# A gated attention loop feeding two experts: the order of three engines taken from tables of steps, two logarithms in one instruction, a state updated in place

## Chip, cores, metric

The kernel runs on one core of one Trainium2 chip. The metric is the device time of one execution in microseconds (us), as the median of the runs shown. A profiled execution has two times of its own: the run's time, and the span of its trace, from which all rows below come.

## What is computed

A complex-gated linear attention over 4 batches, 8 heads, 768 positions and a head size of 48 is followed by a router and a two-layer network per token.

```python
mag = np.sqrt(a_re * a_re + a_im * a_im)
scale = np.minimum(mag, 0.999) / (mag + 1e-06)
for t in range(S):
    # per head: complex state, decayed by the gate, plus the outer product of k and v
    S_re, S_im = ar * S_re - ai * S_im + kv, ar * S_im + ai * S_re
    y[:, :, t] = np.einsum('bhd,bhde->bhe', q[:, :, t], S_re)
...
logits = x @ w_gate + modality_bias[modality_id]      # x: y with the heads side by side, 3072 x 384
e_idx = np.argmax(logits, axis=1)                      # one expert per token, gate_w its softmax weight
h = np.maximum(x[mask] @ w1[e], 0.0)
out[mask] = gate_w[mask, None] * (h @ w2[e])
```

## The kernel before

**Units and pairs.** The 768 positions are cut into G = 6 chunks of 128. A unit n is one chunk of one batch with all heads; there are 24, ordered by chunk, then by batch. Two units of neighbouring batches form a pair x; there are 12. The gate is worked on by pairs, with tiles of 128 x 768 (one half) or 128 x 1536 (both halves); the attention is worked on by units.

**Gate of a pair.** ScalarE squares both parts of the gate (`squares`, L132), VectorE makes their product `tan`, the sign `neg` and the sum of squares; ScalarE takes two logarithms of 128 x 768 (`logs`, L143: the squared modulus into its own tile `lm`, the squared real part in place) and two exponentials (`tangents`, L151: the reciprocal, and `off`, the small correction for the 1e-06); VectorE finishes the tangent and the cut at 0.999. After an arctangent (L164) TensorE sums the angles over the chunk with triangular matrices (`angles`, L167, result `u`), VectorE adds the angle carried from the chunk before and takes the fraction of a turn (`fractions`, L185), ScalarE makes sine and cosine into `css` (`waves`, L205). TensorE sums the logarithms (`sums`, L213, result `ls`), and ScalarE makes the modulus and its reciprocal, `pm` (`moduli`, L222). Row 127 of angle and modulus goes to memory and comes back as the carry `cb` (L182) and as the factor `mt` of the state (L240).

**Attention of a unit.** VectorE makes `qkp` = q,k times `pm`, and `QK` = `qkp` times `css` (`hats`, L243). TensorE turns both into `tKT`, `tQT`; ScalarE copies them out (`turned`, L266). In `inner` (L281) TensorE makes the scores `wp`, VectorE masks them into `W`; TensorE makes the two state additions `up`; VectorE makes `mid` (state after the first half chunk), `U` and the new state `U` x `mt`. In `outer` (L313) TensorE makes `yp` from `W` and the values and from the states; ScalarE copies it to `yT`. In `rows` (L331) TensorE multiplies `yT` by `sel`, which gives rows of tokens and the router's logits (`xw`); ScalarE writes the rows `xr`, VectorE sums the logits `lg`, and a DMA writes the rows to memory (L344).

**Table sets.** Logarithm and exponential are in one table set of ScalarE (EXP), arctangent and sine in another (TRIG); `table` (L103) loads a set. In the loop each pair takes one load of either.

**PSUM.** All of TensorE's results, and those of router and experts, are taken from one pool of four double banks (`pair`, L66). A result's buffer is free when its last reader is done.

**What sets the order.** The loop over turns w (L396 on) writes the steps in program order: pairs run up to five pairs ahead of the units. A planner orders the instructions of each engine from program order, dependences and costs of its own. Only ScalarE's activations and table loads are held in program order (`then`, L98); its copies, and all work of TensorE and VectorE, go where the planner puts them. SP issues nearly all DMAs, in one queue.

**Router and experts.** `beside(w, place)` is called at four places of each turn. It releases one scatter of rows at a time on the GpSimd queue (L636) and, from turn 18 on, parts of the first three expert tiles by a plan of turns and places (`Layers.PLAN`, L745). The router takes the logits in five portions (`takes`), the last after unit 23. After the loop the remaining expert tiles follow (`run`, L887): 12 tiles of 256 rows and one of 128, each with 24 matmuls to `h_ps` in two parts and 8 per 128 rows to `y_ps`. Tiles after the first seven need the places of all rows, so they wait for the last portion.

Of the kernel before, what the change touches and what calls it, by code (L numbers as in the profile page):

```python
# [20 lines left out]
ET = mybir.EngineType  # L21


def gate_loop(nc, ctx, tc, cpool, ident, q, k, v, a_re, a_im, sel, lg, x_rows, make_router, make_layers):
# [71 lines left out]
    chain = []  # L96

    def then(ins):  # L98
        if chain:
            tc.add_manual_dep(ins.ins, chain[-1].ins.name, mybir.DependencyInfo(mybir.DependencyClass.NoSync, mybir.DependencyReason.DATA), reason="order of the table sets")  # L100
        chain.append(ins)

    def table(name):  # L103
        then(nc.scalar.preload_act_table_set(name))  # L104

    def act(*args, **kw):
        then(nc.scalar.activation(*args, **kw))  # L107
# [24 lines left out]
    def squares(x):  # L132
        ab = box.pop(("ab", x))
        sq = el.tile([L, 2, NG, H, D], F32, name="sq", bufs=1)
        act(sq[:], ab, Act.Square)
        tan = el.tile([L, NG, H, D], F32, name="tan", bufs=2)
        nc.vector.tensor_tensor(tan[:], ab[:, 0], ab[:, 1], Alu.mult)
        neg = el.tile([L, NG, H, D], BF16, name="neg", bufs=2)
        nc.vector.tensor_scalar(neg[:], ab[:, 0], 0.0, None, Alu.is_lt)
        nc.vector.tensor_tensor(sq[:, 1], sq[:, 0], sq[:, 1], Alu.add)  # L140
        box["squares", x] = sq, tan, neg

    def logs(x):  # L143

        sq, tan, neg = box["squares", x]
        lm = el.tile([L, NG, H, D], F32, name="lm", bufs=3)
        act(lm[:], sq[:, 1], Act.Ln)
        act(sq[:, 0], sq[:, 0], Act.Ln)
        box["logs", x] = lm

    def tangents(x):  # L151
# [10 lines left out]
        box["lm", x] = lm, off  # L162

    def arctans(x):  # L164
        act(box["tangents", x][0][:], box["tangents", x][0][:], Act.Arctan)

    def angles(x):  # L167

        tan, neg = box.pop(("tangents", x))
        us = pair([L, H, D], "u")  # L170
        for i in range(NG):
            nc.tensor.matmul(us[:, i], turn[:], tan[:, i], start=True, stop=False)  # L172
            nc.tensor.matmul(us[:, i], halfb[:], neg[:, i], start=False, stop=True)
        box["angles", x] = us

    def carries(x):

        g, b = groups[x][0]
        if g:
            cb = el.tile([L, NG, H * D], F32, name="cb")  # L180
            n0 = (g - 1) * B + b
            nc.sync.dma_start(out=cb[:], in_=f_scr[n0:n0 + NG][None].broadcast_to([L, NG, H * D]))  # L182
            box["carry", x] = cb

    def fractions(x):  # L185

        us = box.pop(("angles", x))
        g, b = groups[x][0]
        f = el.tile([L, NG, H, D], F32, name="f")
        r = el.tile([L, NG, H, D], F32, name="r", bufs=1)  # L190
        if g:
            cb = box.pop(("carry", x))
            nc.vector.tensor_tensor(f[:], us, cb[:].rearrange("p i (h d) -> p i h d", d=D), Alu.add)
            nc.vector.tensor_scalar(r[:], f[:], ROUND, -ROUND, Alu.add, Alu.add)
            nc.vector.tensor_tensor(f[:], f[:], r[:], Alu.subtract)
        else:
            nc.vector.tensor_scalar(r[:], us, ROUND, -ROUND, Alu.add, Alu.add)
            box["last"] = nc.vector.tensor_tensor(f[:], us, r[:], Alu.subtract)
# [3 lines left out]
        nc.vector.tensor_scalar(r[:].bitcast(I32), f[:].bitcast(I32), 0x7FFFFFFF, None, Alu.bitwise_and)  # L202
        box["fractions", x] = f, r

    def waves(x):  # L205

        f, r = box.pop(("fractions", x))
        cs = css[:, x % 2]
        act(cs[:, :, :, 1, :], f[:], Act.Sin, scale=2.0 * math.pi)
        act(cs[:, :, :, 0, :], r[:], Act.Sin, scale=-2.0 * math.pi, bias=quarter[:])  # L210
        box["cs", x] = cs

    def sums(x):  # L213

        lm, off = box.pop(("lm", x))
        ls = pair([L, H, D], "ls")
        for i in range(NG):
            nc.tensor.matmul(ls[:, i], half[:], lm[:, i], start=True, stop=False)  # L218
            nc.tensor.matmul(ls[:, i], nhalfb[:], off[:, i], start=False, stop=True)
        box["sums", x] = ls  # L220

    def moduli(x):  # L222
        ls = box.pop(("sums", x))
        pm = el.tile([L, 2, NG, H, D], F32, name="pm")
        act(pm[:, 1], ls, Act.Exp)
        act(pm[:, 0], ls, Act.Exp, scale=-1.0)
        g, b = groups[x][0]
        if g < G - 1:
            n0 = g * B + b
            nc.sync.dma_start(out=m_scr[n0:n0 + NG].rearrange("i h d -> (i h d)")[None], in_=pm[L - 1:L, 1].rearrange("o i h d -> o (i h d)"))  # L230
        box["pm", x] = pm

    def decays(x):

        g, b = groups[x][0]
        if g < G - 1:
            n0 = g * B + b
            mt = mts[x % 4]
            for part in (mt[0:D], mt[64:64 + D]):
                nc.sync.dma_start(out=part, in_=m_scr[n0:n0 + NG].rearrange("i h d -> d i h"))  # L240
            box["mt", x] = mt

    def hats(w):  # L243

        if not 0 <= w < NU or (hats, w) in done:
            return
        done.add((hats, w))
        x, i = w // NG, w % NG
        cs = box["cs", x]
        pm = box["pm", x]  # L250
        qk = box["qk", x]
        qkp = un.tile([L, 2, H, D], F32, name="qkp", bufs=1)
        nc.vector.tensor_tensor(qkp[:], qk[:, :, i], pm[:, :, i], Alu.mult)
        QK = QKs[w % 4]
        wave = cs[:, i].rearrange("p h c d -> p (h c d)")[:, None, :].broadcast_to([L, 2, H * 2 * D])
        twice = qkp[:].rearrange("p a h d -> p (a h) d")[:, :, None, :].broadcast_to([L, 2 * H, 2, D])
        box["hat"] = nc.vector.tensor_tensor(QK[:, :, :, :, 0:D].rearrange("p a h c d -> p (a h c) d"), wave, twice, Alu.mult)  # L257
        box["hats", order[w]] = QK

# [106 lines left out]
    for x in range(2):  # L366
        phase(load_a, x)
# [658 lines left out]
```

## Time and profile before

| | us |
|---|---|
| median of 3 runs | 333.12 (331.14 to 333.34) |
| the profiled execution: its own time | 336.16 |
| the profiled execution: span of its trace | 334.5 |
| busy in the span: TensorE / its weight loads | 264.3 / 208.5 |
| busy in the span: VectorE / ScalarE / GpSimd | 236.4 / 235.2 / 74.9 |

Rows of a timeline give start, duration, engine, line, operation, output and input, count, and in square brackets how long the engine had been idle and what ended it. Rows of windows give a stretch of the span and how long each engine was busy in it, the granted TensorE clock (1.00 is full), the busy share of the 16 DMA engines and the rate. PE is TensorE, PEld its weight loads, DVE is VectorE, ACT ScalarE, POOL GpSimd, SPq the DMA queue of SyncE. A cycle below is the stretch from one EXP load to the next, that is one pair and two units.

### The profile page before, as it was taken

How to read it: one execution, taken by the hardware profiler on the slowest of the kernel's cores; microseconds unless marked ns; L12 is line 12 of the kernel's file. 1: busy time of each engine (PE TensorE's matmuls, PEld its weight loads, DVE VectorE, ACT ScalarE, POOL GpSimd, SP SyncE). 2: the span in 40 equal slices, each digit the busy share in tenths (PEclk: the TensorE clock that was granted, in tenths of full speed). 3: DMA queues.
4: the chain of work that ended last, by engine and by line, in shares of the span. 5: the costliest groups of instructions: out<-in, count | busy, mean ns of one | idle time of the engine just before them, and what ended most of it. 6: DMA issues, size and time to landing. Idle time of an engine off the chain costs nothing.

```text
span 334.5 us, 12364 instructions
## 1 busy us (share of the span) xinstructions
PE 264.3 (79%) x5300; PEld 208.5 (62%) x5300; DVE 236.4 (71%) x437; ACT 235.2 (70%) x291; POOL 74.9 (22%) x110
## 2 busy tenths in 40 slices
PE   0034649779879888978988899999898989899950
PEld 0012438648577776768785878889786767576730
DVE  1619989999998989899898978794452274336510
ACT  2786999999998989979897979534434446432420
POOL 8200000000000000000433323153045148633440
PEclk9999698999989999997999999999999999999995
DMA  8996886969888778695998873927634342644220
GB/s 137 187 187 104 166 168 100 149 91 165 181 182 158 152 142 172 132 181 109 137 240 161 188 159 95 142 77 115 67 65 113 73 129 81 123 94 131 82 90 7
DMA packets 172152, 43.74 MB, mean 131 GB/s; under 512 B 162978, under 2 KB 168484, under 8 KB 172088
## 3 DMA queue, kind: packets, MB, share of 16 engines
q1 hardware_dynamic: 166456, 32.60, 55.7%
q0 software_dynamic: 5632, 10.26, 12.9%
q8 instruction: 43, 0.70, 0.9%
q14 instruction: 21, 0.17, 0.2%
HBM read 33.96 MB, written 9.77 MB: 131 GB/s over the span
## 4 chain that ended last, share of the span: by engine, by line
PE 35%; ACT 24%; DVE 11%; SPq 10%; DMA 8%; issue 6%; POOL 2%; ACTq 1%; POOLq 0%; DVEq 0%
PE h_ps L846 6%; ACT sq L107 5%; SPq L817 4%; PE wp L290 4%; ACT L104 4%; PE y_ps L866 4%; PE up L298 3%; PE yp L327 3%; ACT pm L107 3%; PE xw L336 3%; PE ls L218 3%; PE tQT L274 3%; DMA abs<-in_a_im_dram 2%; PE tKT L274 2%; ACT css L107 2%
## 5 line engine op out<-in xcount | busy, mean ns | idle before, releaser
L636 POOL DMA_INDIRECT x_slots<-xr,to x24 | 31.4, 1307 | 208.6 <-DVE mid L302 147.9
L257 DVE TENSOR_TENSOR QK<-css,qkp 128x1536 f32<-128x1536 f32 x24 | 42.1, 1755 | 0.4
L172 PE MATMUL u<-tan,turn 128*128 128x384 f32 x48 | 22.5, 554 | 23.1 <-ACT tan L107 22.9
L846 PE MATMUL h_ps<-xgT,w1t 128*128 128x256 bf16 (+1 forms) x312 | 35.7, 268 | 1.4 <-DMA xgT<-x_slots 1.4
L866 PE MATMUL y_ps<-w2t,hT 128*128 128x384 bf16 x200 | 35.8, 326 | 1.1 <-ACT hT L849 0.7
L882 POOL DMA_INDIRECT out_dram<-y_sb,idx x25 | 26.7, 1070 | 34.4 <-ACT y_sb L880 16.9
L846 PEld LDWEIGHTS <-w1t 128*128 128x128 bf16 x312 | 29.3, 98 | 6.4 <-issue 1.8
L104 ACT ACT_TABLE_LOAD x25 | 32.1, 1283 | 1.4 <-PEq L1010 0.9
L880 ACT ACTIVATE y_sb<-y_ps,own 128x384 f32<-128x384 f32 x25 | 13.2, 577 | 26.5 <-PE y_ps L866 23.0
L290 PEld LDWEIGHTS wp<-QT,KT 128*64 128x64 f32 x768 | 26.4, 146 | 8.3 <-issue 2.3
L290 PE MATMUL wp<-QT,KT 128*64 128x64 f32 x768 | 30.0, 234 | 2.0 <-ACT ex L107 1.4
L849 ACT ACTIVATE hT<-h_ps 128x1024 bf16<-128x1024 f32 (+1 forms) x20 | 20.0, 1002 | 14.3 <-PE h_ps L846 11.3
L275 ACT COPY KT<-tKT 128x1024 f32<-128x1024 f32 x24 | 24.3, 1012 | 8.1 <-PE tKT L274 5.0
L336 PE MATMUL xw<-sel,yT 128*128 128x104 f32 x192 | 27.0, 284 | 2.1 <-ACT QT L275 1.2
L274 PE MATMUL tKT<-ident,QK 64*128 64x64 f32 x384 | 18.3, 240 | 12.9 <-DVE QK L257 11.4
L298 PE MATMUL up<-V,QK 64*64 64x48 f32 x1408 | 28.1, 221 | 0.0
L866 PEld LDWEIGHTS <-hT 128*128 128x128 bf16 x200 | 18.3, 98 | 14.9 <-issue 2.1
L274 PEld LDWEIGHTS tKT<-ident,QK 64*128 64x128 f32 x384 | 15.0, 148 | 18.7 <-issue 13.9
L298 PEld LDWEIGHTS up<-V,QK 64*64 64x64 f32 x1408 | 25.1, 135 | 1.8 <-DVE lg L342 0.2
L172 PEld LDWEIGHTS u<-tan,turn 128*128 128x128 f32 x48 | 9.0, 214 | 27.4 <-issue 25.6
L336 PEld LDWEIGHTS xw<-sel,yT 128*128 128x128 f32 x192 | 23.4, 191 | 3.9 <-ACT QT L275 1.3
L275 ACT COPY QT<-tQT 128x1024 f32<-128x1024 f32 x24 | 24.5, 1023 | 0.3 <-PE tQT L274 0.3
(153 smaller groups left out, 548.3 us busy)
## 6 DMA issues: line engine op xcount, KB each, us to landing
abs<-in_a_re_dram SPq DMA_DIRECT2D x24, 192.0 KB
abs<-in_a_im_dram SPq DMA_DIRECT2D x24, 192.0 KB
qk<-in_q_dram SPq DMA_DIRECT2D x24, 192.0 KB
qk<-in_k_dram SPq DMA_DIRECT2D x24, 192.0 KB
V<-in_v_dram SPq DMA_DIRECT2D x24, 192.0 KB
cb<-f_scr SPq DMA_DIRECT2D x10, 384.0 KB
x_rows<-xr SPq DMA_DIRECT2D x24, 96.0 KB
abs<-in_moe_w_dram POOLq DMA_DIRECT2D x2, 768.0 KB
```

The source lines that it names most:

```text
L104: then(nc.scalar.preload_act_table_set(name))
L107: then(nc.scalar.activation(*args, **kw))
L172: nc.tensor.matmul(us[:, i], turn[:], tan[:, i], start=True, stop=False)
L257: box["hat"] = nc.vector.tensor_tensor(QK[:, :, :, :, 0:D].rearrange("p a h c d -> p (a h c) d"), wave, twice, Alu.mult)
L274: nc.tensor.transpose(tp[:, s, h], QK[rows_, i, h].rearrange("t c d -> t (c d)"), ident[rows_, rows_])
L275: box["turned QK"] = nc.scalar.copy(to[:], tp)
L290: nc.tensor.matmul(wp[rows_, h, :], KT[:, s, h], QT[:, s, h], start=True, stop=True)
L298: nc.tensor.matmul(up[to_c, s, h], QK[rows_, 0, h, c], V[rows_, h, 0:D], start=True, stop=True)
L336: nc.tensor.matmul(xw[:, j], yT[:, j], sel[:, j], start=True, stop=True)
L636: put = self.nc.gpsimd.indirect_dma_start(out=self.x_slots, out_offset=bass.IndirectOffsetOnAxis(ap=to, axis=0), in_=self.xr[m // 4 * 4][: ...
L846: nc.tensor.matmul(h_ps[:, f // nf, f % nf, :], w1t[:, k, ff * 128:(ff + 1) * 128], xgT[:, k, :], start=(k == 0), stop=(k == KD - 1))
L866: nc.tensor.matmul(y_both[:, s], self.hT[n][:, f, s * 128:(s + 1) * 128], w2t[:, f, :], start=(f == 0), stop=(f == NF - 1))
```

## The change

The functions for phases of a pair and stages of a unit are split into 42 single steps. Two strings name them: FRONT once, with absolute pair and unit numbers, CYCLE for x = 0 to 12, with numbers relative to pair x or unit 2x; steps out of range or already done are skipped. `then` now keeps one chain each for TensorE, ScalarE (copies among them) and VectorE, so the steps of each of these engines run in the order of the strings. What router and experts issue is in no chain, but for activations given to `act`.

Further: both logarithms of a pair are one instruction of 128 x 1536 in place (`ln`; pairs 0 and 1 keep two halves, `la`, `lb`), and the cut at 0.999 reads `sq` and writes `lm`. `U` goes straight into the new state's tile, and `nw` multiplies it in place; the tile `U` is gone. FRONT has 24 matmuls of bf16, 128 x 512, on constants (`warm`), whose result nobody reads, in no chain. The EXP load at the start is no longer written. Gate loads of pair x + 2 are issued when square, product and sign of pair x have been issued; q and k of pair x + 2 after `qkp` of pair x's second unit; values of unit n + 4 after `yV` of unit n; the carry's load right behind the write it reads, and so the load of `mt`. `beside` is called at steps `turn:u.p`, with the same turns and places.

The core of the diff:

```diff
+FRONT = """
+    sq:0 sum:0 tan:0 lb:0 neg:0 la:0 off:0 mn:0 e:0 tan2:0 ls0:0 TRIG warm:24 at:0 u0:0 sq:1 neg:1 sum:1 ls1:0 u1:0 EXP la:1 r:0 tan:1
+    lb:1 f2:0 e:1 ab:0 ep:0 v:0 off:1 tan2:1 em:0 TRIG s:0 qkp:0 mn:1 c:0 qk:1 tan:2 sq:2 QK:0 v:1 sum:2 at:1 tQ:0 ls0:1 EXP u0:1 ln:2
+    qkp:1 cQ:0 neg:2 tK:0 v:2 ls1:1 e:2 QK:1 tan2:2 off:2 cK:0 u1:1 mn:2 sq:3 r:1 sum:3 W:0 f2:1 ep:1 neg:3 em:1 tQ:1 up:0 ln:3 qkp:2
+    e:3 off:3 TRIG s:1 mask:0 mid:0 U:0 tan:3 mn:3 at:2 u0:2 ab:1 u1:2 c:1 tan2:3 sq:4 QK:2 f:2 sum:4 r:2 neg:4 f2:2 at:3 cQ:1 tK:1 v:3
+    cK:1 tan:4 ab:2 s:2 u0:3 u1:3 c:2
+"""
+
+CYCLE = """
+    xw:-1 turn:0.0 f:+3 qkp:+3 r:+3 up:+1 tK:+2 xr:-1 lg:-1 mid:+1 f2:+3 EXP cK:+2 ls0:+2 turn:0.1 ls1:+2 ln:+4 ep:+2 yV:+0 turn:0.2
+    U:+1 QK:+3 em:+2 yS:+0 neg:+5 tan:+5 yT:+0 W:+1 turn:0.3 e:+4 tK:+3 cK:+3 up:+2 turn:1.0 tQ:+2 off:+4 mask:+1 qkp:+4 xw:+0 tan2:+4
+    mid:+2 U:+2 nw:+1 yV:+1 turn:1.1 yS:+1 mn:+4 tQ:+3 turn:1.2 TRIG cQ:+2 ab:+3 xr:+0 W:+2 nw:+0 at:+4 yT:+1 sq:+5 lg:+0 cQ:+3 u0:+4
+    turn:1.3 s:+3 QK:+4 mask:+2 sum:+5 c:+3 u1:+4
+"""
 
...
-    chain = []
-
-    def then(ins):
-        if chain:
-            tc.add_manual_dep(ins.ins, chain[-1].ins.name, mybir.DependencyInfo(mybir.DependencyClass.NoSync, mybir.DependencyReason.DATA), reason="order of the table sets")
-        chain.append(ins)
+    chain = {}
+
+    def then(engine, *made):
+        if engine in chain:
+            tc.add_manual_dep(made[0].ins, chain[engine].ins.name, mybir.DependencyInfo(mybir.DependencyClass.NoSync, mybir.DependencyReason.DATA), reason="order of the steps")
+        chain[engine] = made[-1]
+        return made[-1]
 
     def table(name):
-        then(nc.scalar.preload_act_table_set(name))
+        then("act", nc.scalar.preload_act_table_set(name))
 
     def act(*args, **kw):
-        then(nc.scalar.activation(*args, **kw))
+        return then("act", nc.scalar.activation(*args, **kw))
+
+    def copy(*args):
+        return then("act", nc.scalar.copy(*args))
+
+    def vec(made):
+        return then("vec", made)
 
     order = [(g, b) for g in range(G) for b in range(B)]
...
-    def squares(x):
-        ab = box.pop(("ab", x))
-        sq = el.tile([L, 2, NG, H, D], F32, name="sq", bufs=1)
-        act(sq[:], ab, Act.Square)
-        tan = el.tile([L, NG, H, D], F32, name="tan", bufs=2)
-        nc.vector.tensor_tensor(tan[:], ab[:, 0], ab[:, 1], Alu.mult)
-        neg = el.tile([L, NG, H, D], BF16, name="neg", bufs=2)
-        nc.vector.tensor_scalar(neg[:], ab[:, 0], 0.0, None, Alu.is_lt)
-        nc.vector.tensor_tensor(sq[:, 1], sq[:, 0], sq[:, 1], Alu.add)
-        box["squares", x] = sq, tan, neg
-
-    def logs(x):
-
-        sq, tan, neg = box["squares", x]
-        lm = el.tile([L, NG, H, D], F32, name="lm", bufs=3)
-        act(lm[:], sq[:, 1], Act.Ln)
-        act(sq[:, 0], sq[:, 0], Act.Ln)
-        box["logs", x] = lm
-
-    def tangents(x):
-
-
-        sq, tan, neg = box.pop(("squares", x))
-        lm = box.pop(("logs", x))
+    def parts_read(x):
+
+        if all((part, x) in done for part in ("sq", "tan", "neg")):
+            box.pop(("ab", x))
+            load_a(x + 2)
+
+    def sq(x):
+        box["sq", x] = to = el.tile([L, 2, NG, H, D], F32, name="sq", bufs=1)
+        act(to[:], box["ab", x], Act.Square)
+
...
+    def ln(x):
+
+        sq = box["sq", x]
+        act(sq[:], sq[:], Act.Ln)
+
+    def part_ln(x, i):
+        part = box["sq", x][:, i]
+        act(part, part, Act.Ln)
+
+    def e(x):
+        sq = box["sq", x]
         act(sq[:, 0], sq[:, 0], Act.Exp, scale=-1.0)
-        off = el.tile([L, NG, H, D], BF16, name="off", bufs=2)
-        act(off[:], lm[:], Act.Exp, scale=-0.5, bias=ln_eps[:])
-        nc.vector.tensor_tensor(tan[:], tan[:], sq[:, 0], Alu.mult)
-        nc.vector.tensor_scalar(lm[:], lm[:], 2.0 * math.log(0.999), None, Alu.min)
-        box["tangents", x] = tan, neg
...
+    def mn(x):
+        box["lm", x] = to = el.tile([L, NG, H, D], F32, name="lm", bufs=3)
+        vec(nc.vector.tensor_scalar(to[:], box["sq", x][:, 1], 2.0 * math.log(0.999), None, Alu.min))
+
...
+    def logsum(x, i):
+
+        if i == 0:
+            box["ls", x] = pair([L, H, D], "ls")
+        ls = box["ls", x][:, i]
+        then("pe", nc.tensor.matmul(ls, half[:], box["lm", x][:, i], start=True, stop=False), nc.tensor.matmul(ls, nhalfb[:], box["off", x][:, i], start=False, stop=True))
...
+            for part in (0, 64):
+                nc.sync.dma_start(out=mts[x % 4][part:part + D], in_=m_scr[n0:n0 + NG].rearrange("i h d -> d i h"))
...
+        if i and x + 2 < NX:
+            load_qk(x + 2)
...
-            U = un.tile([C, H, D], F32, name="U")
-            nc.vector.tensor_tensor(U[:], mid[:], ups[1], Alu.add)
-            new = un.tile([C, H, D], F32, name=f"state{b}", bufs=2)
-            nc.vector.tensor_tensor(new[:], U[:], box["mt", (g * B + b) // NG][:, b % NG, :, None].broadcast_to([C, H, D]), Alu.mult)
-            state[b] = new
...
+    def U(n):
+        if more(n):
+            to = box["new", n] = un.tile([C, H, D], F32, name=f"state{order[n][1]}", bufs=2)
+            vec(nc.vector.tensor_tensor(to[:], box["states", n][1][:], box["up", n][:, 1], Alu.add))
+
+    def nw(n):
+        if more(n):
+            to = state[order[n][1]] = box.pop(("new", n))
+            vec(nc.vector.tensor_tensor(to[:], to[:], mts[n // NG % 4][:, n % NG, :, None].broadcast_to([C, H, D]), Alu.mult))
...
+        values(n + 4)
...
+    def step_of(name, n):
+
+        made, end = (A, NX) if name in A else (N_, NU)
+        if 0 <= n < end and (name, n) not in done:
+            done.add((name, n))
+            made[name](n)
+            if name in ("sq", "tan", "neg"):
+                parts_read(n)
...
-    table(EXP)
-    for x in range(2):
-        phase(squares, x)
-        phase(load_a, x + 2)
-        phase(logs, x)
-        phase(tangents, x)
-    table(TRIG)
-    for x in range(2):
-        phase(arctans, x)
-        phase(angles, x)
-    phase(fractions, 0)
-    with tc.issue_after(box["last"].ins):
-        phase(squares, 2)
-    phase(waves, 0)
-    phase(load_qk, 1)
...
+    def run(names, x):
+
+        for step in names.split():
+            name, _, n = step.partition(":")
+            if name == "EXP":
+                if x + 2 < NX:
+                    table(EXP)
+                for made in late:
+                    made(act)
+                late.clear()
+            elif name == "TRIG":
+                if x + 3 < NX:
+                    table(TRIG)
+            elif name == "turn":
+                beside(2 * x + int(n[0]), int(n[2]))
+            elif name == "warm":
+                idle = pair([128, 4, L], "idle")
+                for i in range(int(n)):
+                    nc.tensor.matmul(idle[:, i % 2], nhalfb[:], halfb[:, None, :].broadcast_to([L, 4, L]), start=True, stop=True)
+            elif name in ("qk", "v"):
+                (load_qk if name == "qk" else values)(int(n))
+            else:
+                step_of(name, (x if name in A else 2 * x) + int(n))
+
+    run(FRONT, 0)
+    for x in range(NX + 1):
+        run(CYCLE, x)
     for f in late:
         f(act)
     return open_[-1], layers

```

More of the change, by code (lines that the diff above doesn't have):

```diff
@@ L164, in arctans @@
[L164 to L174, printed above, removed]
+    def parts_read(x):
+        if all((part, x) in done for part in ("sq", "tan", "neg")):
+            box.pop(("ab", x))
+            load_a(x + 2)
@@ L176, in carries @@
     def carries(x):
+        if x < 2 or x >= NX:
+            return
         g, b = groups[x][0]
[L179 to L187, printed above, removed]
-        g, b = groups[x][0]
[L189 to L198, printed above, removed]
+        cb = el.tile([L, NG, H * D], F32, name="cb")
@@ L331, in rows @@
[L331 to L342 removed]
+            nc.sync.dma_start(out=m_scr[n0:n0 + NG].rearrange("i h d -> (i h d)")[None], in_=box["pm", x][L - 1:L, 1].rearrange("o i h d -> o (i h d)"))
```

325 lines of the change are left out of this document (143 added, 182 removed).

## The prediction

> **What bounds the kernel now.** I read the table loads on ScalarE first, to cut the span into cycles, then the busy time of each engine in the seven cycles from one EXP load to the next (57.89 to 177.08).
>
> ```profile
> 57.89:73.51 15.62, 11.66 (x233) 8.45 (x232) 15.62 (x23) 15.36 (x18) 0.00 (x0) 1.00 0.78 117
> 73.51:88.12 14.61, 13.73 (x376) 11.13 (x374) 14.53 (x24) 14.52 (x19) 0.00 (x0) 1.00 0.90 174
> 88.12:103.71 15.59, 13.11 (x368) 11.31 (x369) 15.42 (x23) 15.50 (x19) 0.00 (x0) 0.89 0.93 181
> 103.71:121.70 17.99, 15.81 (x415) 12.98 (x415) 16.45 (x24) 16.56 (x20) 0.00 (x0) 1.00 0.76 145
> 121.70:139.56 17.86, 16.02 (x417) 13.15 (x417) 16.40 (x28) 16.57 (x20) 0.00 (x0) 1.00 0.75 146
> 139.56:158.89 19.33, 16.41 (x420) 13.94 (x420) 18.23 (x49) 16.82 (x21) 0.24 (x1) 0.91 0.76 143
> 158.89:177.08 18.19, 16.95 (x422) 13.99 (x422) 17.21 (x31) 16.47 (x21) 7.03 (x6) 1.00 0.99 179
> sum 119.19, PE 103.69 PEld 84.95 DVE 113.86 ACT 111.79 POOL 7.27; mean PE 14.81 PEld 12.14 DVE 16.27 ACT 15.97 POOL 1.04
> ```
>
> The columns after the length are TensorE, its weight loads, VectorE, ScalarE, GpSimd, granted clock, DMA share, GB/s. Three engines are nearly full at once: VectorE 113.86 and ScalarE 111.79 of 119.19, TensorE 103.69. The first three cycles are short because they hold less unit work (233 to 376 matmul records against 415). The next are the full ones: near 18 with 16.5 of work on each of two engines, so 1.4 per cycle is handover. One such handover is a wait of TensorE for a free PSUM buffer (it needs no `yT` to turn `tQT`):
>
> ```profile
> 115.86 0.71 PE L274 MATMUL tQT<-ident,QK 64*128 64x64 f32 x16 [1.28 <-ACT yT L328]
> ```
>
> Behind the cycles the bound is another engine:
>
> ```profile
> 177.08:237.00 59.92, 54.64 (x1419) 46.09 (x1419) 46.39 (x114) 41.96 (x55) 18.10 (x15) 1.00 0.73 133
> 237.00:290.00 53.00, 50.56 (x641) 39.21 (x636) 22.22 (x65) 24.34 (x34) 25.39 (x25) 1.00 0.35 91
> ```
>
> TensorE is busy 91% and 95%: there it sets the pace, and the change removes no matmul. So I cost three stretches: up to the EXP load of cycle 0 (57.89), seven cycles to the EXP load of cycle 7 (177.08), and the rest.
>
> **The front.** ScalarE is the engine to add up, from these steps (start to next start):
>
> ```profile
> 7.82 1.48 ACT L107 ACTIVATE sq<-abs 128x1536 f32<-128x1536 f32 x1 [5.59 <-DMA abs<-in_a_im_dram]
> ...
> 57.89 1.28 ACT L104 ACT_TABLE_LOAD   x1
> ```
>
> ```profile
> 109.24 1.51 ACT L107 ACTIVATE pm<-ls 128x768 f32<-128x768 f32 x2 [0.38 <-PE ls L219]
> 110.64 0.85 ACT L107 ACTIVATE lm<-sq 128x768 f32<-128x768 f32 x1
> 111.37 1.72 ACT L107 ACTIVATE sq<-sq 128x768 f32<-128x768 f32 x2
> 112.99 0.92 ACT L107 ACTIVATE off<-lm,ln_eps 128x768 bf16<-128x768 f32 x1
> 113.93 1.28 ACT L104 ACT_TABLE_LOAD   x1
> 115.22 0.58 ACT L328 COPY yT<-yp 128x512 f32<-128x512 f32 x1
> ...
> 116.08 0.86 ACT L107 ACTIVATE tan<-tan 128x768 f32<-128x768 f32 x1
> 116.82 1.01 ACT L275 COPY KT<-tKT 128x1024 f32<-128x1024 f32 x1
> 117.71 1.03 ACT L275 COPY QT<-tQT 128x1024 f32<-128x1024 f32 x1
> 118.62 0.88 ACT L107 ACTIVATE css<-f 128x768 f32<-128x768 f32 x1
> 119.36 0.95 ACT L107 ACTIVATE css<-r,quarter 128x768 f32<-128x768 f32 x1
> 120.19 1.50 ACT L107 ACTIVATE sq<-abs 128x1536 f32<-128x1536 f32 x1
> 121.70 1.28 ACT L104 ACT_TABLE_LOAD   x1
> ```
>
> FRONT puts on ScalarE 5 squares at 1.5 (7.5), 4 half logarithms at 0.73 (2.9), 2 whole ones taken as a square (3.0), 4 reciprocals at 0.81 (3.2), 4 `off` at 0.94 (3.8), 4 arctangents at 0.74 (3.0), 3 sines and 3 cosines at 0.74 and 0.83 (4.7), 2 x 1.40 for `pm`, 4 copies at 0.90 (3.6) and 7 table loads at 1.29 (9.0): 43.5. Seven, because five are written and no load of the EXP set stands ahead of pair 0's logarithms any more: I take one to be put in before the logarithm and one before the exponential. From 7.82 that gives 51.3. Laying VectorE's steps beside it, I find the last sine due about 1.3 too early for its `f2`, so 52.6 instead of 57.89, if nothing else is late. FRONT has one copied unit and one `yT` less behind it, which the cycles below make up.
>
> [...]
>
> `warm` has no row. Its nearest are a bf16 matmul of 384 columns and the first sums of angles, cold and warm:
>
> ```profile
> L866 PE MATMUL y_ps<-w2t,hT 128*128 128x384 bf16 x200 | 35.8, 326 | 1.1 <-ACT hT L849 0.7
> ```
>
> ```profile
> 21.90 1.62 PE L172 MATMUL u<-tan,turn 128*128 128x384 f32 x2 [21.90 <-ACT tan L107]
> ...
> 26.39 0.81 PE L172 MATMUL u<-tan,turn 128*128 128x384 f32 x2
> ```
>
> 24 x 0.326 x 512/384 = 10.4 at most, on an engine that had nothing before 21.90; the constants are ready early, the first `u` is due near 17. If it keeps the clock up, two sums gain 0.8 each, which ScalarE's order hides. If the planner puts it behind the first `ls` instead, near 14.5, `u` comes up to 8 late, of which up to 5 reach ScalarE. I take 0, and keep -1 to +5.
>
> **The cycle.** VectorE does the same work in another order. What an order can save there stands in four rows:
>
> ```profile
> 107.95 0.55 DVE L139 TENSOR_SCALAR neg<-abs 128x768 bf16<-128x768 f32 x1
> 108.42 0.55 DVE L194 TENSOR_SCALAR r<-f 128x768 f32<-128x768 f32 x1
> 109.00 0.96 DVE L195 TENSOR_TENSOR f<-f,r 128x768 f32<-128x768 f32 x1
> 110.00 0.56 DVE L202 TENSOR_SCALAR r<-f 128x768 int32<-128x768 int32 x1
> ```
>
> `r` follows `neg` after 0.47, but `f` follows `r`, which it reads, after 0.58, and the next reader comes 1.00 after an instruction of 0.96. A reader directly behind its writer pays about 0.1. CYCLE has one such pair (`mid` and `U` of the second unit) where the old order has seven or eight: 16.45 becomes 15.7. The state in place changes no shape: 0, with no reason for more than 0.1 either way. Router work comes on top: 18.23 and 17.21 in the two cycles with a portion, so 2.6, and 0.5 for its setup, 0.45 per cycle: 16.15.
>
> ScalarE loses one start per pair: 0.73 + 0.81 against 1.5 or less, 0.1 taken (bounds 0 and 0.15). With the waits gone, and their edges (0.2), its 16.56 becomes 16.2 to 16.3. TensorE has 15.81 or less.
>
> Do the orders fit into each other? I laid the steps of one cycle side by side, ScalarE dense. Every copy finds its matmuls done (nearest: the first `cK`, 0.15 after its transposes; TensorE has about 0.9 per cycle in hand). `mask` of the first unit comes 0.1 behind its scores. At most four PSUM buffers are alive, but four allocations per cycle (`yV` and `tQ` of the second unit, the next scores, `u`) take the fourth. So 16.3 is the floor. I add 0.4, a third of VectorE's present idle time in the full cycles (1.3 each): 16.7. Seven cycles from 52.6 end at 169.5, against 177.08: **-7.6**.
>
> On SP, the loads of `mt` and of the carry now stand right behind the writes they read, and gate, q, k and value loads queue behind them.
>
> ```profile
> SPq L240 <- DMA m_scr<-pm: 3.4, 2, 1.9
> ```
>
> Two waits of 1.9 per cycle are 3.8 of SP's time. Gate loads have over a cycle in hand, and q and k too, so I cost it at 0; without that cover it is up to 3.8 a cycle. Bytes: 17.99 x 145 GB/s is 2.6 MB a cycle, 156 GB/s at 16.7, and the rows show 181 at a share of 0.93. That fits.
>
> **The rest.** At its EXP load of cycle 7 the new order has done two TensorE steps that the old one had not, `up` of unit 15 and `xw` of unit 13:
>
> ```profile
> L336 PE MATMUL xw<-sel,yT 128*128 128x104 f32 x192 | 27.0, 284 | 2.1 <-ACT QT L275 1.2 <-ACT sq L107 1.0
> L298 PE MATMUL up<-V,QK 64*64 64x48 f32 x1408 | 28.1, 221 | 0.0
> ```
>
> 27.0/24 + 28.1/24 = 2.3, on the engine that bounds the rest: **-2.3**. The rows of unit 23 now stand ahead of the parts of expert tiles of turn 24, which helps the one late transfer of the tail:
>
> ```profile
> PE h_ps L846 <- DMA xgT<-x_slots: 1.4, 2, 0.8
> ```
>
> Half of it: **-0.7**. Sum -10.6: 336.16 becomes 325.6 for a profiled execution; that one stands 3.04 over the median, so the median goes from 333.12 to **322.5**.
>
> **Rivals.** *Faster throughout:* cycles at their floor (166.7, -10.4), and TensorE denser in the rest as well. It idles 5.3 and 2.4 there; without half of that, 3.9, and with -2.3, the sum is -16.6: 316.5. For: nothing but matmuls bounds that stretch. Against: the planner still places what the experts add.
>
> *Handovers stay:* three fixed orders hand every delay on, and VectorE stays idle for 7%, as in the four full cycles. 16.3/0.93 = 17.5 a cycle, 175.1 at cycle 7, -2.0 - 2.3: 328.8. For: the old planner, free to choose, did no better. Against: it put readers directly behind writers.
>
> *Slower, by PSUM:* each of the four allocations that take the last buffer waits for ScalarE or VectorE, and in a fixed order TensorE can do nothing else. At 0.57 each, half of the 1.28 seen, a cycle is 19.0, cycle 7 begins at 185.6, +8.5 - 2.3: 339.3. It makes the kernel slower than before from 18.1 a cycle, a wait of 0.35 each, and by over 1% from 18.6. For: the 1.28 is such a wait already. Against: my layout frees each buffer just in time.
>
> *It does not do what it says:* what router and experts issue is in no table, so the planner may set it where a step is due. That is in the 0.4, or in the second rival.
>
> **How the numbers follow.** Forecast 0.60 (own range 318 to 327.5), faster throughout 0.14, handovers stay 0.17, PSUM 0.09. About 1%, 3.3 us, is what a measurement here can tell from no change. Faster by more than 1% (under 329.8): 0.60 + 0.14 + half of 0.17 = 0.82. Within 1%: the other half and a little of PSUM, 0.10. Slower 0.08. The range reaches from below the first rival's 316.5 over the second to the beginning of the slow side: 314.5 to 331.5; a late `warm` lies in it.
>
> **What would show it.** Right: the EXP load of cycle 0 near 52.6 and that of cycle 7 near 169.5; ScalarE's logarithms at 1.4 to 1.5 each; two more table loads before 17; no wait of `tQT` for `yT`; VectorE over 95% busy in the cycles. Wrong: waits of TensorE for PSUM readers in every cycle, cycles of 17.5 or more, a first EXP load later than 55, or VectorE waiting for loads.

## The result, and the profile after

The median went from 333.12 to 329.18 (7 runs each, 325.58 to 330.83 after): ratio 0.9876, 95% interval 0.9828 to 0.9923. The forecast was 322.5. So the change made the kernel faster, by 3.9 where 10.6 were forecast. Run again beside the kernel before (`after_again` below), it was 1.0 faster (ratio 0.9960, with an interval up to 0.9998), so how much it gains is not settled. (Ratios here leave disturbed executions out and medians do not, so the two need not agree to the last digit.) The profiled execution after took 328.19, with a span of 326.6.

First the front, from the timeline of the changed kernel: start, duration, engine, and in brackets how long the engine was idle and what ended it.

```profile
8.07 1.28 ACT L124 ACT_TABLE_LOAD   x1 [8.07 <-DMA abs<-in_a_im_dram]
9.36 1.48 ACT L124 ACTIVATE sq<-abs 128x1536 f32<-128x1536 f32 x1
10.86 1.28 ACT L124 ACT_TABLE_LOAD   x1
13.75 1.28 ACT L124 ACT_TABLE_LOAD   x1
16.30 7.32 PE L454 MATMUL idle<-halfb,nhalfb 128*128 128x512 bf16 x24
23.45 0.81 PE L211 MATMUL u<-tan,turn 128*128 128x384 f32 x2
25.27 0.81 ACT L124 ACTIVATE pm<-ls 128x768 f32<-128x768 f32 x1 [1.41 <-PE ls L260]
26.08 0.96 DVE L234 TENSOR_SCALAR r<-u 128x768 f32<-128x768 f32 x1 [4.85 <-PE u L211]
31.65 1.48 ACT L124 ACTIVATE sq<-abs 128x1536 f32<-128x1536 f32 x1 [1.06 <-issue]
56.10 0.84 ACT L124 ACTIVATE css<-f 128x768 f32<-128x768 f32 x1 [1.60 <-DVE f L240]
58.39 1.28 ACT L121 ACT_TABLE_LOAD   x1
```

The last row is the EXP load of cycle 0: 58.39, where 52.6 was forecast and before had 57.89. Three table loads were put in, not two, and the first stands behind the data it did not need. `warm` runs from 16.30, behind the first `ls`, and the first `u` follows it at 23.45; VectorE had waited 4.85 for it.

Then the cycles, from the busy time of each engine between EXP loads (TensorE, its weight loads, VectorE, ScalarE, GpSimd, clock, DMA share, GB/s), and the matmul-bound stretches behind:

```profile
74.61:90.82 16.21, 14.55 (x376) 11.81 (x377) 16.07 (x29) 16.15 (x20) 0.00 (x0) 1.00 0.78 130
107.03:123.24 16.21, 16.15 (x423) 13.39 (x418) 15.85 (x24) 16.15 (x19) 0.00 (x0) 1.00 0.89 179
139.46:156.71 17.25, 16.11 (x433) 13.28 (x424) 17.22 (x47) 16.41 (x21) 4.86 (x4) 1.00 0.84 171
156.71:176.26 19.55, 17.55 (x422) 14.55 (x418) 18.30 (x39) 16.58 (x20) 6.16 (x6) 0.91 0.95 184
sum 117.87, PE 110.05 PEld 90.28 DVE 115.73 ACT 113.77 POOL 11.02; mean PE 15.72 PEld 12.90 DVE 16.53 ACT 16.25 POOL 1.57
```

```profile
176.26:236.20 59.94, 54.83 (x1438) 46.39 (x1431) 45.79 (x105) 39.90 (x51) 15.47 (x12) 0.96 0.73 120
236.20:289.20 53.00, 52.40 (x612) 40.30 (x611) 24.07 (x66) 26.80 (x38) 27.46 (x29) 0.98 0.39 102
```

Five cycles last 16.21 or 16.22 each, with ScalarE busy 16.15: it is full. Only the sixth, which VectorE fills with a router portion, and the seventh, with another portion and a clock of 0.91, are longer. Seven cycles took 117.87; 116.9 was forecast.

### The profile page after: what moved, and what is told of

Its sections match the earlier page's. It is cut to its first block, busy times and chain, and to the rows that moved or that the text cites. A ratio compares the mean times of both kernels' runs of the same rounds, so it can differ in the third digit from the quotient of the medians.

```text
span 326.6 us, 12449 instructions
## 1 busy us (share of the span) xinstructions
PE 273.1 (84%) x5324; PEld 211.6 (65%) x5324; DVE 232.5 (71%) x437; ACT 235.5 (72%) x283; POOL 74.2 (23%) x110
## 4 chain that ended last, share of the span: by engine, by line
PE 30%; DVE 18%; issue 15%; DMA 13%; ACT 12%; POOL 4%; SPq 4%; POOLq 0%; ACTq 0%; DVEq 0%
PE h_ps L853 10%; PE y_ps L873 7%; ACT sq L124 4%; DMA xgT<-x_slots 3%; POOL x_slots L643 3%; DMA abs<-in_a_im_dram 2%; PE idle L454 2%; PE yp L358 2%; DVE QK L298 2%; PE xw L368 2%; DVE hT L858 2%; DMA x_slots<-xr,to 2%; DVE qkp L290 2%; PE up L323 1%; DMA abs<-in_a_re_dram 1%
## 5 line engine op out<-in xcount | busy, mean ns | idle before, releaser
L853 PE MATMUL h_ps<-xgT,w1t 128*128 128x256 bf16 (+1 forms) x312 | 37.2, 273 | 5.6 <-DMA xgT<-x_slots 5.6
L260 PE MATMUL ls<-lm,half 128*128 128x384 f32 x48 | 22.2, 546 | 13.8 <-DVE ef L708 13.8
L124 ACT ACTIVATE sq<-sq 128x768 f32<-128x768 f32 (+1 forms) x26 | 28.3, 1098 | 0.1
L315 DVE TENSOR_TENSOR W<-wp,mask 128x512 f32<-128x512 f32 x24 | 16.4, 684 | 16.1 <-PE wp L311 16.1
L311 PE MATMUL wp<-QT,KT 128*64 128x64 f32 x768 | 27.1, 224 | 0.4 <-ACT KT L127 0.3
L211 PE MATMUL u<-tan,turn 128*128 128x384 f32 x48 | 22.6, 555 | 5.6 <-ACT tan L124 4.8
L368 PEld LDWEIGHTS xw<-sel,yT 128*128 128x128 f32 x192 | 24.3, 195 | 3.6 <-ACT QT L127 0.7
L302 PE MATMUL tQT<-ident,QK 64*128 64x64 f32 x384 | 18.1, 236 | 9.3 <-DVE QK L298 8.2
```

What stands on the lines that cost most here:

```text
L124: return then("act", nc.scalar.activation(*args, **kw))
L211: then("pe", nc.tensor.matmul(u, turn[:], box["tan", x][:, i], start=True, stop=False), nc.tensor.matmul(u, halfb[:], box["neg", x][:, i], ...
L311: then("pe", *[nc.tensor.matmul(wp[rows_, h, :], KT[:, p, h], QT[:, p, h], start=True, stop=True) for h in range(H) for p, rows_ in enumer ...
L368: then("pe", *[nc.tensor.matmul(to[:, j], yT[:, j], sel[:, j], start=True, stop=True) for j in range(J)])
L853: nc.tensor.matmul(h_ps[:, f // nf, f % nf, :], w1t[:, k, ff * 128:(ff + 1) * 128], xgT[:, k, :], start=(k == 0), stop=(k == KD - 1))
```

## The experiments

All ratios are against the kernel before, run beside it on the same chip. The experiments came in three batches; those of one batch share the runs of the kernel before, and ratios compare best within a batch. The row of the change in the table below is from the result above. The base W named below is `exp_warm_first`.

**Before once more.** `before_again` is the old kernel unchanged.

> The kernel before, unchanged, to see how one profiled execution stands to the median. Theory 'outlier': the first profiled execution of before (span 334.5, time 336.16) was a slow one, by its cycles of 17.9 to 18.2 and its granted clock of 0.89 to 0.91 in two of seven cycles; a second profile then has a span 2.5 to 3.5 shorter (331 to 332) and the EXP load of cycle 7 at 174 to 175 or the rest shorter. Rival 'profiling adds': a profiled execution of this kernel always stands some 3 above the median; span again 334 to 335, EXP load of cycle 7 at 177. The ratio against itself must be 1.00; its interval tells what a measurement can see.

Measured: 333.55, ratio 1.0008 (0.9979 to 1.0038); a second profile with a span of 331.6 instead of 334.5.

```profile
sum 118.97, PE 104.10 PEld 84.23 DVE 113.30 ACT 112.14 POOL 6.77; mean PE 14.87 PEld 12.03 DVE 16.19 ACT 16.02 POOL 0.97
```

Here the seven cycles run from 58.31 to 177.28, and the rest takes 154.3 (first profile: 157.4). So the first profile was an outlier, as the theory has it, but by its rest and not by its cycles. The prediction had subtracted its 3.04 from the time, but measured against it the rest looks 3 better than it is. The working below uses the second profile.

**Which part of the front cost what.** Four kernels, each one or two words of FRONT:

```diff
 exp_at_head, exp_no_warm, exp_warm_first (W):
-    sq:0 sum:0 tan:0 ...
+    EXP sq:0 sum:0 tan:0 ...            (exp_warm_first: EXP warm:24 sq:0 ...)
 exp_no_warm, exp_warm_first, warm_first_only:
-    ... ls0:0 TRIG warm:24 at:0 u0:0 ...
+    ... ls0:0 TRIG at:0 u0:0 ...
 warm_first_only:
+    warm:24 sq:0 sum:0 tan:0 ...
```

> One word more in FRONT: the EXP set is loaded ahead of the first square. It takes the three inserted table loads of the front (8.07, 10.86, 13.75) off ScalarE's path: 1.3 by the first, 2.6 by the others. Theory 'ScalarE's chain sets the front, and what comes early stays early': EXP load of cycle 0 at 54.5 instead of 58.39, the whole 3.9 shorter, ratio against before 0.976. Rival 'TensorE's late sums and VectorE set the front': warm still stands in front of the sums, its end moves with ls; the waits of ScalarE for TensorE and VectorE grow, EXP load of cycle 0 at 56.5 to 58, ratio 0.983 to 0.988. Rival 'lost behind': EXP load at 54.5, but the end moves by less than 1.5, because the first expert tile's loads do not come earlier.

> The EXP set at the head of FRONT, and warm taken out (24 matmuls of constants, nothing that the output needs). Theory 'warm stands in the way': the sums u of pair 0 start when tan is ready (near 15.0 instead of 19.6 with warm), VectorE's 4.85 and ScalarE's 1.41 of waiting go, EXP load of cycle 0 at 52.5 to 53.5, ratio 0.970 to 0.973. Rival 'warm earns its place by the clock': sums and transposes run at 1.6 and 1.1 instead of 0.8 and 0.7 through the front, EXP load within 0.7 of that of exp_at_head.

> The EXP set at the head of FRONT, and warm written right behind it, so that the 24 matmuls of constants stand ahead of the first sums on TensorE (constants are ready at 5.8; 24 at 0.31 to 0.63 end at 13 to 20). Theory 'the place of warm is the cost, the clock is worth little': EXP load of cycle 0 within 0.7 of exp_no_warm when warm ends before 14. Rival 'the clock is worth it': 0.7 to 1.6 earlier than exp_no_warm, since the first sums run at 0.8. If the 24 start cold and end at 20, it is no better than exp_at_head.

> Against the changed kernel only one word moves: warm stands at the head of FRONT; the EXP set is not written there, so the three inserted table loads come back. With exp_warm_first (first EXP load of a cycle at 52.56) and exp_at_head (55.81) it completes a square of four. Theory 'two costs that add': the loads cost 2.6 to 3.9 of ScalarE's path whatever warm does: EXP load of cycle 0 at 55.2 to 56.5, ratio 0.975 to 0.979. Rival 'warm was the whole cost': 52.6 to 53.5, ratio 0.967 to 0.970, since the loads hide in VectorE's and TensorE's work.

| | EXP load of cycle 0 | median | ratio |
|---|---|---|---|
| the change | 58.39 | 329.18 | 0.9876 (0.9828 to 0.9923) |
| exp_at_head | 55.81 | 329.50 | 0.9886 (0.9836 to 0.9936) |
| exp_no_warm | 53.49 | 328.56 | 0.9796 (0.9738 to 0.9854) |
| exp_warm_first | 52.56 | 323.82 | 0.9673 (0.9617 to 0.9730) |
| warm_first_only (another chip, before at 337.1) | 57.44 | 333.14 | 0.9834 (0.9766 to 0.9902) |

The timelines of `exp_at_head`, then of `exp_warm_first`:

```profile
13.96 6.21 PE L454 MATMUL idle<-halfb,nhalfb 128*128 128x512 bf16 x24
22.63 0.96 DVE L234 TENSOR_SCALAR r<-u 128x768 f32<-128x768 f32 x1 [4.68 <-PE u L211]
55.81 1.28 ACT L121 ACT_TABLE_LOAD   x1
```

```profile
5.88 8.00 PE L454 MATMUL idle<-halfb,nhalfb 128*128 128x512 bf16 x24 [5.88 <-POOL nhalfb L74]
18.50 0.96 DVE L234 TENSOR_SCALAR r<-u 128x768 f32<-128x768 f32 x1 [0.42 <-PE u L211]
52.56 1.28 ACT L121 ACT_TABLE_LOAD   x1
```

With the loads gone but `warm` where it was, VectorE still waits 4.68 for `u`: the front ends 2.6 earlier, not 3.9, between theory and rival, and the total did not follow: in its profile the first cycle takes 18.52 (see the last section) and the seventh 20.95. With `warm` moved as well, in time in which TensorE had nothing to do, the wait is 0.42 and the front ends at 52.56. Moving `warm` alone brings 0.95, since the loads (at 8.00, 10.80 and 13.69 in its timeline) then hold ScalarE; the loads alone bring 2.6; both bring 5.8. Each hid behind the other, so the theory that they add is wrong, and so is its rival (52.6 to 53.5). The 0.95 is from the other chip, where the front of `early_weights` is 0.8 longer than on this one (53.41, below 52.60); with that much added the two still fall short of 5.8. `warm` ahead is worth 0.6 to 0.9 of front over no `warm` at all (52.85 and 52.56 in two profiles of W). That `exp_no_warm` is behind W by 0.0123 of the ratio, some 4, is more than that: its rest took 155.0 against 151.5. Part of that are stops of TensorE like those of the last section: its profile has four of over 1 (1.02, 1.09, 1.56 and 1.83), two profiles of W have one each (1.43, 1.20). What else was not settled.

**Is that the whole miss?** The second batch had been on a slower chip, so four kernels were run together on one.

> The changed kernel as it is, beside the next three in one call, since the chip of the second call was slower as a whole (before at 337.1, where the first call had 333.5) and ratios of different calls do not compare. Expected: EXP load of cycle 0 at 58.0 to 58.8 again, ratio against before 0.985 to 0.990. If the ratio depends on the chip, as the theory 'a denser TensorE stream pays more for late instructions and a lower clock' says, it is nearer to 1 on the slower chip: 0.990 to 1.000 where before is above 336.

> exp_warm_first once more, beside the changed kernel. Theory 'the front's miss is the three table loads and the place of warm': 5.0 to 6.0 shorter than the changed kernel in the same call (ratio 0.016 to 0.020 lower), EXP load of cycle 0 at 52.5 to 53.5. Rival 'a lucky run of the first call': less than 2.5 shorter (0.008).

The change: 331.99, ratio 0.9960 (0.9923 to 0.9998). W: 322.70, ratio 0.9716 (0.9667 to 0.9765): 9.3 shorter in the same batch, more than expected. Their profiles differ by 5.3 in the front (58.11 to 52.85), by 3.6 in the seven cycles (119.87 to 116.27) and by 0.8 behind them. Of the 3.6, 2.3 stand in cycle 0, which ran at a clock of 0.72 in this profile of the change and at 1.00 in its first one, and 1.3 in the seventh. The ratio of the change did move towards 1, beyond the 0.990 expected, though its chip was not the slow one (before at 332.95); so the theory that ties this to the chip is not borne out.

**The expert stretch.** In the change TensorE waits for the first expert tile. Its timeline shows why (POOL is GpSimd's queue):

```profile
210.61 1.13 POOL L787 DMA_DIRECT2D css<-in_moe_w_dram  x1 [17.40 <-DVE xr L587]
...
216.30 2.27 POOL L643 DMA_INDIRECT x_slots<-xr,to  x1 [0.30 <-issue]
222.32 0.39 SPq L823 DMA_DIRECT2D own<-x_slots  x1
232.27 0.37 PE L853 MATMUL h_ps<-xgT,w1t 128*128 128x256 bf16 x1 [3.95 <-DMA xgT<-x_slots]
233.81 2.29 PE L853 MATMUL h_ps<-xgT,w1t 128*128 128x256 bf16 x10 [1.16 <-DMA xgT<-x_slots]
```

The scatters wait for routing weights whose exponential comes only behind an EXP load; in the kernel before, such an exponential could also go at odd turns once no TRIG load followed. `early_weights` is W with

```diff
             elif name == "TRIG":
+                for made in late:
+                    made(act)
+                late.clear()
                 if x + 3 < NX:
```

> exp_warm_first, and the routing weights that wait for the EXP set are also written ahead of each TRIG load (there the EXP set is still in), not only behind an EXP load. The exponential of the portion of units 12 to 15 then comes near 194.5 instead of 203.14, its row scatters can begin at 202 to 203.5 (places are known at 202.13) instead of 207.59, the loads of the first expert tile 4 earlier. Theory 'the wait for the first tile is on the path of the matmul-bound rest': TensorE's wait of 4.41 for xgT goes, with it some 1.5 of matmuls at half clock behind it; ratio 0.967 goes to 0.950 to 0.956. Rival 'it is given back later' (the second and third tile's loads, or the tail's transfers, bound the end): the wait of 4.41 goes, the end moves by less than 1.5, ratio 0.963 to 0.968.

> early_weights once more, beside exp_warm_first in the same call. In its first profile TensorE's wait of 4.41 for the first expert tile was gone, but the stretch from the EXP load of cycle 7 to the end took 157.5 instead of 151.5, on another chip. Theory 'the wait was on the path': ratio 0.010 to 0.016 below warm_first_again. Rival 'it is given back': within 0.005 of it, and the wait gone all the same.

On the slower chip it gave 333.28, ratio 0.9891 (0.9834 to 0.9948), outside both forecasts (0.950 to 0.956, 0.963 to 0.968); W was not run there. Beside W it gave 321.55, ratio 0.9612 (0.9540 to 0.9684): 1.2 less by the medians, 0.0104 by the ratios (its own rests on three of six runs), with intervals that overlap a little. In its profile (322.24, 0.7 above its median) the first tile starts without a wait, and a later one waits instead:

```profile
224.58 1.48 PE L856 MATMUL h_ps<-xgT,w1t 128*128 128x256 bf16 x12
...
274.43 0.27 PE L856 MATMUL h_ps<-xgT,w1t 128*128 128x256 bf16 x1 [0.99 <-DVE w2t L814]
...
276.91 4.23 PE L856 MATMUL h_ps<-xgT,w1t 128*128 128x256 bf16 x22 [1.36 <-DMA xgT<-x_slots]
```

So some of the wait of over 4 was probably on the path, but part of it is given back some 50 later, where the matmuls also run slower (4.23 for 22; W has 2.56). W waits for `xgT` there too (0.96 and 0.54 in its two profiles), and so does `early_weights` on the slower chip (1.05, its matmuls at 2.56), so only some of this waiting comes with the edit. How much it gains stays between 1 and 3.5. This version has the lowest median measured, and W, which differs by the three lines, is close.

**VectorE's order alone.** `vector_order_free` is W with only ScalarE's chain kept:

```diff
-        if engine in chain:
+        if engine == "act" and engine in chain:
```

> exp_warm_first without the fixed order of VectorE and TensorE: the steps are written in the same sequence, but only ScalarE is held to it. TensorE's order comes out the same, so what is tested is VectorE's. Theory 'a written order that keeps readers from directly behind their writers is what fits 16.2': some seven pairs at 0.1 come back, VectorE takes 16.5 or more of a cycle, cycles of 16.6 to 17.5, ratio 0.972 to 0.985. Rival 'ScalarE's order alone makes the cycle': cycles stay at 16.2 to 16.3, ratio 0.965 to 0.969.

> vector_order_free once more, beside exp_warm_first in the same call. Its first profile had the EXP load of cycle 0 at 55.23, and seven cycles of 120.65 where early_weights had 120.66 on the same chip. Theory 'VectorE's written order is worth something in the front alone': ratio 0.005 to 0.009 above warm_first_again, EXP load of cycle 0 near 55, cycles at 16.2 except where TensorE stands. Rival 'it makes the cycle': 0.015 or more above, most cycles over 16.6. Rival 'nothing': within 0.004.

334.67, ratio 0.9890 (0.9827 to 0.9952), on the slower chip and outside both ranges; 326.43, ratio 0.9793 (0.9737 to 0.9850), beside W. That is 0.0077 above W, the size that the theory of a gain in the front alone has, with the front at 55.67 (W: 52.85). That the gain is in the front alone is not shown: on the slower chip the seven cycles are as long as those of `early_weights` (120.65 and 120.66), but in this profile, 4.0 above its median, they take 123.21 against W's 116.27. Two of them:

```profile
107.11:123.53 16.42, 15.81 (x427) 13.14 (x422) 15.77 (x24) 16.34 (x20) 0.00 (x0) 1.00 0.92 161
...
158.22:178.88 20.66, 19.05 (x433) 16.05 (x427) 17.29 (x39) 16.54 (x20) 6.14 (x6) 0.83 0.92 176
```

In the fourth cycle, the first row, VectorE is busy 15.77 without a written order; W has 15.86 and 15.88 there with it. So the smaller VectorE work of a cycle does not need the chain. It can still come from the order: the planner, which now follows the sequence of the steps, puts one reader directly behind its writer in this cycle (`QK` behind `qkp`), as the chain does (`U` behind `mid`). A run with the old order in the new kernel was not made.

**One logarithm alone.** In the kernel before:

```diff
-        act(lm[:], sq[:, 1], Act.Ln)
-        act(sq[:, 0], sq[:, 0], Act.Ln)
+        act(sq[:], sq[:], Act.Ln)
```

> The kernel before, with both logarithms of a pair in one instruction and lm taken from sq by VectorE: one part of the change alone, twelve ScalarE starts fewer. Theory 'a start saved is 0.05 to 0.1': at most 1.2 in all, hidden where ScalarE waits: ratio 0.996 to 1.000. Rival 'a good part of the gain is the merged logarithms': 0.99 or less. Rival 'slower': sq stays in use until VectorE has taken its minimum, and the next squares wait for it: 1.005.

335.14 against 337.1, ratio 0.9948 (0.9915 to 0.9982), so 1.8 by the ratio, somewhat over the 0.1 per pair of the first theory, whose 0.996 lies in the interval. Beside the change's own gain (0.0124 and 0.0040 in ratio) that is no small part; whether it adds to the order's was not run.

## Why the prediction was wrong

Set against the second profile of before, whose time of 333.19 is close to the median:

| | before | forecast | the change | W (first, second) |
|---|---|---|---|---|
| EXP load of cycle 0 | 58.31 | 52.6 | 58.39 | 52.56, 52.85 |
| seven cycles | 118.97 | 116.9 | 117.87 | 117.82, 116.27 |
| rest | 154.3 | 151.3 | 150.3 | 151.5, 150.1 |
| span | 331.6 | 320.8 | 326.6 | 321.9, 319.2 |

The forecast's rest is 154.3 less the 2.3 and 0.7 of the prediction. The profiled execution of the change lies 1.0 under its median. 5.8 + 1.0 - 1.0 + 1.0 is 6.8, the miss of 6.7. In the second profile of the change the front is 5.5 late and the cycles 3.0, of which 2.3 are cycle 0 at the lower clock; the miss of that batch is 9.5.

**The front failed, at the step "I take 0" for `warm` and at the loads.** The prediction named what came ("if the planner puts it behind the first `ls` instead, `u` comes up to 8 late, of which up to 5 reach ScalarE") and priced it at nothing: `u` came at 23.45 where 17 was meant. The loads were three, and the first could not run ahead, since it was put in with the square and waited for the square's data; the sum had two, and began with the square at 7.82. ScalarE's waits behind them (1.41, 1.06, 0.88, 1.60 and 0.49 in its timeline) add to 5.4 where 1.3 was allowed: with the third load (1.3) and the start 0.25 later that is 5.7 of the 5.8. W, which differs from the change in these two things alone, reaches the forecast's 52.6 and comes to 323.82 and 322.70. Yet W does not pay the two loads that the forecast had paid for, 2.6. In their place stand waits of ScalarE that the sum lacked: W has 1.03, 0.63, 1.60 and 0.50, 3.8 in all, 2.5 over the 1.3. Two errors cancel there, and the agreement is luck to that extent.

**The cycles came out near, partly by luck.** The floor of 16.3 by ScalarE came out as 16.21, and the 0.4 per cycle added for late handovers was not there. Another term filled its place. The prediction spread the router's work on VectorE over seven cycles, where it stays under ScalarE's floor; but it stands in two, and there VectorE is the fullest engine. The sixth takes 17.25, and the seventh takes 17.97 at the full clock in W's second profile:

```profile
151.15:169.12 17.97, 16.12 (x422) 13.21 (x418) 17.76 (x39) 16.57 (x19) 7.10 (x6) 1.00 0.98 195
```

Over 16.21 that is 1.0 and 1.8, together as much as seven times 0.4. The 19.55 of the change is 1.6 longer still, with a longer stop of TensorE (1.83; W's is 1.20) and the half clock (0.50) behind it, a cause which no step of the prediction has. `tQT` waits for no `yT`, the logarithms take 1.49, VectorE is busy 98 to 100% of five cycles. Rival "handovers stay" falls, and so does the one by PSUM: in no cycle does TensorE wait regularly for a reader of PSUM. VectorE's 15.7 came out as 15.86. That its order is the reason fits: the cycle of before shown in the prediction has six readers directly behind their writers (seven or eight were counted), CYCLE has one, and five times 0.1 is most of the 0.6 between 16.45 and 15.86. No run isolates it.

**The rest came near in sum, by other terms.** Two steps less were to take 2.3 of work off TensorE, and the late transfer was to halve (-0.7). From the waits of the change:

```profile
PE h_ps L853 <- DMA xgT<-x_slots: 5.6, 3, 3.9
```

That was 1.4 in before. The weights that the scatters need do not come later (their exponential runs at 207.61, in the second profile of before at 211.61); but TensorE reaches the first tile at 228.04 instead of 238.78, ahead of its transfer. The rest is 4.0 shorter all the same: TensorE is busy 132.6 of it and idle 17.7, against 133.7 and 20.6 in the second profile of before. So 1.0 of work went, not 2.3, and it stood less elsewhere, as the rival "faster throughout" had it. Two stops like those of the last section, 1.35 and 1.22, stand in that profile of before, and none of over 1 in the change; the other waits were not taken apart.

## What to carry to other kernels

Write a table load where it is wanted. The first one that FRONT left out was put in with the square and stood behind the square's wait for data (8.07 in the change, the square at 9.36); written at the head it ran at 0.95 in `exp_at_head`, ScalarE then still waited 5.57 for that data, and the square began at 7.79. Work that is only there to keep an engine's clock up must be held ahead of the work that it serves, by order or dependence: unplaced, `warm` became the wait (4.85 for `u` in the change), and at the head of W that wait was 0.42, with the first `ls` at 0.81 where `exp_no_warm` has 1.62. And when two delays overlap, taking away one shows little (2.6 and 0.95 here, 5.8 together), so remove both before judging either.

## What the runs showed of the hardware

**TensorE stopped at fixed places of its program.** The seventh cycle of the change, 19.55 long, holds this stop, inside one run of matmuls that needs nothing new. First the change, then `exp_no_warm`, then `before_again`:

```profile
165.83 0.37 PE L323 MATMUL up<-V,QK 64*64 64x48 f32 x10 [1.83 <-issue]
...
166.77 1.80 PE L368 MATMUL xw<-sel,yT 128*128 128x104 f32 x8
168.51 1.13 PE L352 MATMUL yp<-W,V 64*64 64x64 f32 x32
```

```profile
159.24 0.22 PE L358 MATMUL yp<-QT,mid 128*48 128x64 f32 x1 [1.56 <-issue]
```

```profile
168.81 0.34 PE L321 MATMUL yp<-W,V 64*64 64x64 f32 x7 [1.76 <-issue]
```

Counted along TensorE's program (an fp32 matmul is two rows in the trace, each with its weight load: for the 24 that L211 of the change issues, its profile has 48 rows and 48 weight loads, for the 24 in bf16 there 24 and 24), they stand at instruction 5781, 5525 and 5531, and in W at 5783: all 149 to 155 past a multiple of 256. Counted with the records that the timeline leaves out (semaphores, branches), the fit is exact: the first late record is number 5826 in the change and in W, 5570 in the other two, each 194 past a multiple of 256. The fourteen profiles have 22 idle times of TensorE of over 1.0 that no engine and no data transfer ends, and all 22 stand at such a place. `exp_no_warm`, whose program is 48 instructions shorter, stalls 256 earlier in it and so at another step. The page of the profile has a queue for instructions:

```profile
q8 instruction: 44, 0.72, 0.9%
```

0.72 MB in 44 packets is 16.4 KB each; spread over the 256 instructions from one place to the next that is 64 bytes an instruction, an estimate from these two numbers. In the change one of 42 such places stops TensorE for over 0.6; in `exp_no_warm` it is eight of 41. The trace also has the packets themselves: in the change the 22nd packet of 16384 bytes on that queue lands at 164.50, and the matmuls from record 5826 on, which is 22 times 256 and 194, start at 165.83. In all 22 stops the last packet landed has the number of the multiple, and landed 1.2 to 1.7 before TensorE went on. In the change no place, with a stop or without, was passed less than 1.33 after the packet of its number had landed. So the stops fit a wait for that packet; this is read from the order of the two, and no run changed when a packet came. Why it came late is open: whether dense data transfers delay it (their share in the cycle was 0.95) was not tried.

**The clock halved behind short gaps.** Behind the stop of 1.83 the granted clock is 0.50 from 167.06 to 170.47, `xw` takes 1.80 (1.03 to 1.15 at the full clock) and the clock of the cycle is 0.91. In the first cycle of `exp_at_head` the clock fell with two waits, of 1.13 and 1.31 within 3.8:

```profile
58.17 1.15 PE L311 MATMUL wp<-QT,KT 128*64 128x64 f32 x32 [1.13 <-ACT KT L127]
60.63 1.11 PE L302 MATMUL tKT<-ident,QK 64*128 64x64 f32 x16 [1.31 <-DVE QK L298]
61.67 1.96 PE L323 MATMUL up<-V,QK 64*64 64x48 f32 x64
```

```profile
55.81:74.33 18.52, 16.08 (x335) 13.99 (x338) 16.02 (x23) 16.46 (x19) 0.00 (x0) 0.72 0.81 146
```

The cycle takes 18.52 instead of 16.21. The same happened in the second profile of the change (18.55, clock 0.72) and not in its first, so it comes and goes from one execution to the next. The second profile of W has the same two waits (1.01 and 1.31) and kept the full clock. What differs is how they fall. In every profile the granted clock changes only at whole multiples of 3.41 from its other changes (in the change, counted from 20.29, behind 3, 5, 8, 10, 43, 44, 62, 64 and 88 of them). Cut at these borders, the stretches around the two waits are, first in `exp_at_head`, then in W:

```profile
56.66:60.08 3.42, 1.53 (x46) 1.24 (x41) 3.42 (x5) 3.41 (x4) 0.00 (x0) 1.00 1.00 228
60.08:63.49 3.41, 2.86 (x80) 2.75 (x80) 3.41 (x6) 3.41 (x6) 0.00 (x0) 0.50 0.66 129
```

```profile
53.34:56.75 3.41, 2.01 (x68) 1.66 (x60) 3.41 (x6) 3.40 (x4) 0.00 (x0) 1.00 0.98 237
56.75:60.16 3.41, 2.48 (x97) 2.32 (x98) 3.41 (x5) 3.41 (x6) 0.00 (x0) 1.00 0.85 166
```

With TensorE busy 1.53 of one stretch the clock fell in the next; with 2.01 and 2.48 it did not. In the change it was 1.58 ahead of the fall behind the stop of 1.83. These stretches show no one limit: at 1.98 it fell in W's first profile, at 1.86 it stayed in `exp_no_warm`. In none of them was TensorE idle throughout.
